# The guard's count and its comparison, issued two steps behind the sums that they use

## The chip, the cores and the metric

The kernel runs on one core of one Trainium2 chip. The metric is the device time of one execution in microseconds; lower is better. Engines are named as in the profile: PE (TensorE matmul) and PEld (its weight loads), DVE (VectorE), ACT (ScalarE), POOL (GpSimd), SP (SyncE, which issues most DMAs).

## The reference

Three blocks follow each other: an attention with a window and sink positions, a gated feed-forward block with a short convolution along the sequence, and an attention with four experts of which two are weighted per position.

```python
scores = np.where(is_sink | in_window, scale * q @ k.T, -1e9)   # 2 x 8 heads, 768 positions, 64 wide
x = softmax(scores) @ v                                          # n_sink 4, window 128
h = np.maximum(x @ w_in, 0.0)                                    # 512 -> 1024
conv_out = sum(conv_w[k] * shifted(h, k - 1) for k in range(3))
y = h * sigmoid(conv_out) @ w_out                                # 1024 -> 512
for e in range(4):                                               # causal attention of each expert
    a = softmax(causal(scale * (y @ wq[e]) @ (y @ wk[e]).T))
    out += weight_of_the_two_best(y @ w_gate, e) * (a @ (y @ wv[e]) @ wo[e])
```

`w_in`, `conv_w` and `w_out` come as 64-bit floats, the rest as 32-bit floats. `n_sink` and `window` are inputs too.

## The kernel before, in words

All work is laid out for 128 partitions. The first attention goes over two batches of 6 row tiles and 4 pairs of heads (lines 450 to 640). The feed-forward block follows in steps: for batch 0 three chunks of 256 positions in two halves of the hidden tiles, for batch 1 two chunks of 384 positions over 8 hidden tiles `f`. The last block makes queries, keys and values (lines 922 and 991) and then goes over 6 row tiles and 2 pairs of experts for each batch (lines 1040 to 1136).

One step of the feed-forward block in batch 1 is this chain, which is spread over four steps of the program (`LAGM`):

- `m1_H` (line 768): 12 matmuls of 128x386 into one PSUM buffer `psB`; ACT takes it out with the relu (L774) and multiplies the middle tap (L776).
- `m1_conv`: DVE adds the two outer taps (L785, L786), ACT takes the tanh (L788).
- `m1_gate`, one step later: DVE multiplies (L794), ACT copies a rounded half `g[0]` (L800). `m1_rest`, another step later: POOL makes the remainder `g[1]` (L806).
- `m1_Y` (line 822), three steps behind `m1_H`: 12 matmuls of 128x384 that add `w_out` times `g` into four PSUM buffers, which are held over the 8 hidden tiles.

In each step the program order is given by the string `ORD1`: `rest`, `H`, `gate`, `Y`, `conv` and then `z.misc`, which is the function `misc` of `mlp_phase`. Each engine works through its own list in program order. There are 8 PSUM buffers `psB`, handed out in turn; with four held by `m1_Y`, four go round.

The 64-bit weights are turned into 32-bit floats on the chip by a short sequence that is right only for magnitudes under a bound. While it reads the weights, ACT sums their scaled magnitudes into the columns of the tile `guard`, 128 x 17 (L340). When the last weights are done, at step `w0` of the feed-forward block, `misc` calls `narrow`: DVE compares the 17 columns with the bound (L189) and adds up each row into `g` (L190), PE adds up the 128 rows with a matmul of `g` against a column of ones (L192, 1x1 output), and DVE compares the result with 128 x 17 and multiplies by the verdict on `n_sink` and `window` (L193) into `flag`. The flag is read once, at the end of the program: if it is 0, a general version of the whole program runs as well.

In the same step `misc` then lays out the buffers for the weights of the last block and issues their first load (L888, one in each of 8 steps).

Of the kernel before, what the change touches and what calls it, by code (L numbers as in the profile page):

```python
# [89 lines left out]
class Kernel:  # L90
# [94 lines left out]
    def narrow(self):  # L185

        nc = self.nc
        g, ok = self.sm(1, "g"), self.guard
        nc.vector.tensor_scalar(ok, ok, GUARD, None, op0=ALU.is_lt)  # L189
        nc.vector.tensor_reduce(g, ok, axis=AX.X, op=ALU.add)  # L190
        ps = self.psB()[0:1, 0:1]
        nc.tensor.matmul(ps, g, self.ones, start=True, stop=True)  # L192
        nc.vector.scalar_tensor_tensor(self.flag[0:1], ps, float(P * (2 * NF + 1)), self.inside[0:1, 0:1], op0=ALU.is_ge, op1=ALU.mult)  # L193

    def indices(self):
# [669 lines left out]
    def mlp_phase(self, start):  # L865
        nc = self.nc
        self.m1h, self.m1g = {}, {}
        hf = NF // 2 if self.halves else NF
        steps = [(0, c, f) for f0 in range(0, NF, hf) for c in range(NCH) for f in range(f0, f0 + hf)]
        steps1 = [(1, c, f) for c in range(NT // TPC[1]) for f in range(NF)]  # L870
        w0 = NSTEP + NF // 2

        def misc(i):
            self.tail_step()
            self.background(BG2 // 2)
            if i == w0 and self.halves:
                self.narrow()
            if i == w0:
                hi = self.Kt([P, NKC, WQKV], F32R, "wqh")
                self.wq_ = ([hi[:, :, lo:up] for lo, up in WCOLS], [self.Rt([P, NKC, up - lo], s="wql") for lo, up in WCOLS])  # L880
            if w0 <= i < w0 + 2 * NKC:
                n = i - w0
                raw = self.Wt([P, DM], s="raw")
                kc = n // 2
                groups = (2,) if n % 2 else (0, 1)
                lo, up = WCOLS[groups[0]][0], WCOLS[groups[-1]][1]
                raw = raw[:, : up - lo]
                nc.sync.dma_start(raw, self.wqkv[kc * P : (kc + 1) * P, lo:up])  # L888
                self.wraw[n] = [(raw[:, WCOLS[g][0] - lo : WCOLS[g][1] - lo], *(w[g][:, kc] for w in self.wq_)) for g in groups]
            if w0 + 2 <= i < w0 + 2 + 2 * NKC:  # L890
                for part in self.wraw.pop(i - w0 - 2):
                    self.hilo_later(*part)

        def more(i):
            self.tail_step()
            self.background(BG2 // 2)

        def phase(start, steps, lags):
            def each(fn):
                return lambda i: fn(*steps[i])  # L900

            conv, gate, rest, Y = lags
            st = {"rest": (rest, each(self.m1_rest)), "gate": (gate, each(self.m1_gate)), "conv": (conv, each(self.m1_conv)),
                  "H": (0, each(self.m1_H)), "Y": (Y, each(self.m1_Y))}
            return lambda names: (start, len(steps), [st[n] for n in names.split()], 1)

        n0 = start + len(steps)
        total = len(steps) + len(steps1)
        z = {"more": (0, more), "misc": (0, misc)}
        return (phase(start, steps, LAGM[0]), phase(n0, steps1, LAGM[1]),  # L910
                lambda names: (start, total, [z[n] for n in names.split()], 1), start + total)
# [422 lines left out]
```

## Time and profile before

| | |
|---|---|
| time, median of 3 runs | 377.04 us (376.21 to 377.78) |
| the profiled execution's own time | 375.66 us |
| its span, from the first to the last instruction | 373.7 us |
| TensorE's granted clock over the span, mean | 0.995 of full speed |
| PE busy | 360.1 us (96%), 2974 instructions |
| PEld busy | 331.8 us (89%) |
| DVE busy | 276.4 us (74%) |
| ACT busy | 257.8 us (69%) |
| POOL busy | 118.8 us (32%) |

Times in the trace are counted from the start of the span. A group of matmuls is read best by the start of its first and the start of the next group's first, since ends of matmuls are modelled. The clock is given as the share that the throttle granted: 1.00 is 2.4 GHz, 0.50 is 1.2 GHz. An idle time in square brackets stands before the instruction and names what ended it.

### The profile page before, as it was taken

To read this page: it belongs to the slowest core of one execution; us is meant where nothing else is said; L and a number is where in the kernel's file an instruction comes from. 1 tells how busy PE (TensorE), PEld (TensorE's weight loads), DVE (VectorE), ACT (ScalarE), POOL (GpSimd) and SP (SyncE) were. 2 spreads that over 40 slices of the span, in tenths; PEclk is the share of its full clock that TensorE was granted. 3 is DMA by queue.
4 is the path that set the end of the run, shared out by engine and by line. 5 is a ranking of instruction groups with operands and counts; after the bars stand their busy time and mean duration, and the time that the engine had idled before them with its cause. 6 is when DMAs were issued, how large, how long until landed. Compare 5 with 4: busy or idle time off the path is not lost.

```text
span 373.7 us, 8472 instructions
## 1 busy us (share of the span) xinstructions
PE 360.1 (96%) x2974; PEld 331.8 (89%) x2974; DVE 276.4 (74%) x843; ACT 257.8 (69%) x731; POOL 118.8 (32%) x224
## 2 busy tenths in 40 slices
PE   7999999899999999999699999999999999999995
PEld 5687777899889999999699999999999899978984
DVE  5689898999887987777837577457678697668731
ACT  4999998767877776446435655449869687839841
POOL 7013111444332352843512212410025134505320
PEclk9999999999999999999989999999999999999999
DMA  7944865363332300001101101000000000101012
GB/s 181 356 140 121 251 203 172 114 198 114 119 109 81 91 29 31 16 14 31 42 16 46 39 3 53 5 1 2 2 0 4 0 30 30 56 3 59 30 59 92
DMA packets 20402, 27.49 MB, mean 74 GB/s; under 512 B 2080, under 2 KB 12416, under 8 KB 20352
## 3 DMA queue, kind: packets, MB, share of 16 engines
q1 hardware_dynamic: 19120, 26.22, 22.0%
q10 hardware_dynamic: 1232, 0.66, 0.9%
q8 instruction: 25, 0.41, 0.4%
q14 instruction: 25, 0.20, 0.2%
HBM read 23.68 MB, written 3.19 MB: 72 GB/s over the span
## 4 chain that ended last, share of the span: by engine, by line
PE 67%; DVE 19%; ACT 6%; issue 3%; POOL 2%; DMA 1%; ACTq 0%; DVEq 0%; POOLq 0%
PE psB L822 12%; PE psB L768 10%; PE psB L991 9%; PE psB L1107 5%; PE psB L1083 5%; PE psB L922 5%; PE psB L1131 4%; PE psB L588 4%; PE psB L485 3%; DVE P L487 3%; PE psB L546 3%; PE psB L1054 2%; PE psB L1053 2%; DVE ht L786 2%; DVE ht L785 2%
## 5 line engine op out<-in xcount | busy, mean ns | idle before, releaser
L822 PE MATMUL psB<-g,wouthf 128*128 128x256 f32 (+1 forms) x320 | 68.5, 304 | 0.2 <-POOL g L806 0.2
L1071 POOL TENSOR_SCALAR P<-P,r 128x256 f32<-128x256 f32 (+5 forms) x48 | 30.1, 641 | 79.8 <-DVE r L1069 32.7
L490 ACT ACTIVATE P<-P,nm 128x260 f32<-128x260 f32 (+2 forms) x96 | 46.4, 486 | 10.9 <-DVE nm L487 10.8
L822 PEld LDWEIGHTS psB<-g,wouthf 128*128 128x128 f32 x320 | 52.8, 188 | 0.9 <-POOL g L806 0.7
L822 PE MATMUL psB<-g,woutlf 128*128 128x256 f32 (+1 forms) x160 | 48.4, 303 | 0.0
L1060 ACT ACTIVATE P<-P,nm 128x256 f32<-128x256 f32 (+5 forms) x48 | 32.1, 670 | 13.4 <-DVE nm L1059 7.8
L768 PE MATMUL psB<-xh,winhf 128*128 128x258 f32 (+1 forms) x128 | 40.8, 319 | 0.1
L768 PE MATMUL psB<-xh,winlf 128*128 128x258 f32 (+1 forms) x128 | 38.5, 301 | 0.0
L768 PE MATMUL psB<-xl,winhf 128*128 128x258 f32 (+1 forms) x128 | 38.5, 301 | 0.0
L778 POOL TENSOR_SCALAR ht<-ht,cw 128x256 f32<-128x256 f32 x24 | 15.1, 630 | 62.4 <-ACT ht L774 56.2
L1056 DVE CUSTOM_DVE_ANT_0 P<-psB,causal 128x384 f32<-128x384 f32 (+3 forms) x64 | 30.2, 502 | 5.7 <-PE psB L1054 5.3
L806 POOL TENSOR_TENSOR g<-t,g 128x384 fp32r<-128x384 f32 x16 | 17.0, 1065 | 48.4 <-ACT g L800 36.3
L822 PEld LDWEIGHTS psB<-g,woutlf 128*128 128x128 f32 x160 | 30.1, 188 | 0.0
L546 PE MATMUL psB<-ident,P 128*128 128x128 f32 x176 | 29.1, 281 | 0.4 <-ACT P L490 0.2
L991 PE MATMUL psB<-yh,wqh 128*128 128x256 f32 x96 | 27.2, 283 | 0.0
L991 PE MATMUL psB<-yh,wql 128*128 128x256 f32 x96 | 27.0, 281 | 0.0
L991 PE MATMUL psB<-yl,wqh 128*128 128x256 f32 x96 | 26.9, 281 | 0.0
L502 ACT COPY PT<-psB 128x512 f32<-128x512 f32 (+1 forms) x48 | 25.5, 531 | 0.8 <-PE psB L546 0.8
L768 PEld LDWEIGHTS psB<-xh,winhf 128*128 128x128 f32 x128 | 24.8, 194 | 0.6 <-ACT ht L774 0.4
L788 ACT ACTIVATE t<-t 128x384 f32<-128x384 f32 x16 | 8.4, 525 | 24.3 <-DVE t L786 24.3
L768 PEld LDWEIGHTS psB<-xl,winhf 128*128 128x128 f32 x128 | 24.7, 193 | 0.0
L768 PEld LDWEIGHTS psB<-xh,winlf 128*128 128x128 f32 x128 | 24.6, 192 | 0.0
(198 smaller groups left out, 1030.5 us busy)
## 6 DMA issues: line engine op xcount, KB each, us to landing
raw<-in_w_in_dram SPq DMA_DIRECT2D x8, 512.0 KB, 4.7
raw<-in_w_out_dram SPq DMA_DIRECT2D x8, 512.0 KB, 3.4
v<-in_v_dram SPq DMA_DIRECT2D x12, 256.0 KB, 4.5
R<-rD SPq DMA_DIRECT2D x24, 128.0 KB, 3.1
out_dram<-ot SPq DMA_DIRECT2D x11, 256.0 KB, 2.0
k<-in_k_dram SPq DMA_DIRECT2D x7, 260.0 KB, 3.9
q<-in_q_dram SPq DMA_DIRECT2D x6, 256.0 KB, 4.0
k<-in_k_dram SPq DMA_DIRECT2D x2, 520.0 KB
```

What stands on the lines that cost most here:

```text
L490: nc.scalar.activation(Pt[:, j, :N], Pt[:, j, :N], AF.Exp, bias=nmx[:, j : j + 1], scale=-1.0, accum_out=sums[:, j : j + 1])
L502: self.nc.scalar.copy(dst, src)
L546: nc.tensor.transpose(ps[:, j, c, :], Pt[:, j, c0 : c0 + P], self.ident)
L768: nc.tensor.matmul(ps[:, : n + 2], w[:, f, kc, :], x[kc], start=(i == 0), stop=(i == len(ops) - 1))
L822: nc.tensor.matmul(self.m1y[d // per][:, d % per, :], w[:, f, d, :], g[k], start=(first and i == 0 and d % per == 0), stop=(last and i == ...
L922: nc.tensor.matmul(ps[:, :NVG], y[:, kc, ts_], w[2][:, kc], start=(i == 0), stop=(i == len(ops) - 1))
L991: nc.tensor.matmul(ps, w[which][:, kc, cols], y[:, kc, :], start=(i == 0), stop=(i == len(ops) - 1))
L1056: nc.vector.tensor_tensor_reduce(out=Pt[:, lo:hi], in0=ps[:, : hi - lo], in1=mask, scale=-1.0, scalar=BIG, op0=ALU.add, op1=ALU.min, accum ...
L1060: nc.scalar.activation(Pt[:, :N], Pt[:, :N], AF.Exp, bias=nm[:, 0:1], scale=-1.0, accum_out=sums[:, j : j + 1])
L1071: nc.gpsimd.tensor_scalar(Ps[j][:, :N], Ps[j][:, :N], r[:, j : j + 1], 1.0, op0=ALU.mult, op1=ALU.mult)
L1083: nc.tensor.transpose(ps[:, s, :], Ps[j][:, c * P : (c + 1) * P], self.ident)
L1107: nc.tensor.matmul(o[j * D : (j + 1) * D, p, :], self.v2[(b, c)][:, e * D : (e + 1) * D], where[(j, c)], start=(c == 0), stop=(c == qt), s ...
```

## The change

`narrow` keeps the two DVE instructions and remembers `g`. The matmul and the comparison become a function of their own, `decide`, which `misc` calls at step `w0 + 2`. Nothing is added or left out: the numbers of instructions on every engine stay as they were. All lines behind the edit count 5 more in the changed file (7 more behind the second edit).

```diff
         nc.vector.tensor_scalar(ok, ok, GUARD, None, op0=ALU.is_lt)
         nc.vector.tensor_reduce(g, ok, axis=AX.X, op=ALU.add)
+        self.within = g
+
+    def decide(self):
+
+        nc = self.nc
         ps = self.psB()[0:1, 0:1]
-        nc.tensor.matmul(ps, g, self.ones, start=True, stop=True)
+        nc.tensor.matmul(ps, self.within, self.ones, start=True, stop=True)
         nc.vector.scalar_tensor_tensor(self.flag[0:1], ps, float(P * (2 * NF + 1)), self.inside[0:1, 0:1], op0=ALU.is_ge, op1=ALU.mult)
...
             if i == w0 and self.halves:
                 self.narrow()
+            if i == w0 + 2 and self.halves:
+                self.decide()
```

PE's list at step `w0` before: the end of one `m1_Y` group, the count's matmul, the start of the next `m1_H` group.

```order
L822 MATMUL psB_2741<-g_2682,wouthf 128x384
L822 MATMUL psB_2741<-g_2681,woutlf 128x384
L192 MATMUL psB_2801<-ones,g_2798 1x1
L768 MATMUL psB_2811<-xh_1244,winhf 128x386
L768 MATMUL psB_2811<-xl_1246,winhf 128x386
```

PE's list at the same place in the changed kernel.

```order
L827 MATMUL psB_2741<-g_2682,wouthf 128x384
L827 MATMUL psB_2741<-g_2681,woutlf 128x384
L773 MATMUL psB_2808<-xh_1244,winhf 128x386
L773 MATMUL psB_2808<-xl_1246,winhf 128x386
L773 MATMUL psB_2808<-xh_1244,winlf 128x386
```

And two steps on, where the count's matmul now stands.

```order
L827 MATMUL psB_2741<-g_2778,wouthf 128x384
L827 MATMUL psB_2741<-g_2779,wouthf 128x384
L827 MATMUL psB_2741<-g_2778,woutlf 128x384
L197 MATMUL psB_2883<-ones,g_2798 1x1
L773 MATMUL psB_2891<-xh_1244,winhf 128x386
L773 MATMUL psB_2891<-xl_1246,winhf 128x386
```

On PE the count's matmul has moved behind 48 other matmuls: the `m1_H` group (now into `psB_2808`), the `m1_Y` group on `g_2719`, the next `m1_H` group and the `m1_Y` group on `g_2778`.

DVE's list before, from the last taps ahead of the two sums on (`t` and `h` are tiles of one hidden tile `f` each).

```order
L786 SCALAR_TENSOR_TENSOR t_2774<-h_2773,cw,t_2774 128x384
L189 TENSOR_SCALAR guard<-guard 128x17
L190 TENSOR_REDUCE g_2798<-guard 128x1
L193 SCALAR_TENSOR_TENSOR flag<-psB_2801,c_831 1x1
L794 SCALAR_TENSOR_TENSOR t_2774<-t_2774,h_2773 128x384
```

DVE's list in the changed kernel.

```order
L791 SCALAR_TENSOR_TENSOR t_2774<-h_2773,cw,t_2774 128x384
L189 TENSOR_SCALAR guard<-guard 128x17
L190 TENSOR_REDUCE g_2798<-guard 128x1
L799 SCALAR_TENSOR_TENSOR t_2774<-t_2774,h_2773 128x384
L790 SCALAR_TENSOR_TENSOR t_2822<-h_2821,cw,t_2822 128x384
L791 SCALAR_TENSOR_TENSOR t_2822<-h_2821,cw,t_2822 128x384
L799 SCALAR_TENSOR_TENSOR t_2822<-t_2822,h_2821 128x384
L790 SCALAR_TENSOR_TENSOR t_2861<-h_2860,cw,t_2861 128x384
L791 SCALAR_TENSOR_TENSOR t_2861<-h_2860,cw,t_2861 128x384
L198 SCALAR_TENSOR_TENSOR flag<-psB_2883,c_831 1x1
L799 SCALAR_TENSOR_TENSOR t_2861<-t_2861,h_2860 128x384
```

On DVE the two sums stay where they were; the comparison has moved behind six instructions. On ACT, POOL and SP the order of the instructions is unchanged.

## Rows read from the trace of the kernel before

**Rows 1.** The page: engines over the span, and the granted clock in 40 slices.

```profile
PE 360.1 (96%) x2974; PEld 331.8 (89%) x2974; DVE 276.4 (74%) x843; ACT 257.8 (69%) x731; POOL 118.8 (32%) x224
...
PEclk9999999999999999999989999999999999999999
```

**Rows 2.** The chain of waits that ended last, around 186 us: start us, us, what.

```profile
185.34 0.18 DVE g L190
185.66 0.19 PE psB L192 x2
185.85 3.70 PE psB L768 x12
189.54 2.10 PE psB L822 x12
191.64 2.14 PE psB L768 x12
```

**Rows 3.** PE's waits over the span: line, releaser, total us, times, longest us.

```profile
PE psB L192 <- DVE g L190: 2.9, 1, 2.9
PE psB L515 <- DVE su L498: 1.8, 4, 1.0
```

**Rows 4.** Timeline of DVE: start us, us, engine, line, operation, tiles, count, [idle before].

```profile
180.02 1.54 DVE L786 SCALAR_TENSOR_TENSOR t<-h,cw,t 128x384 f32<-128x384 f32 x1
...
185.34 0.17 DVE L190 TENSOR_REDUCE g<-guard 128x1 f32<-128x17 f32 x1
...
191.47 1.28 DVE L786 SCALAR_TENSOR_TENSOR t<-h,cw,t 128x384 f32<-128x384 f32 x1
```

**Rows 5.** Timeline of PE, the same columns: first and last matmuls of the groups.

```profile
178.14 0.34 PE L822 MATMUL psB<-g,woutlf 128*128 128x384 f32 x1
178.32 0.34 PE L768 MATMUL psB<-xh,winhf 128*128 128x386 f32 x1
...
180.45 0.51 PE L822 MATMUL psB<-g,wouthf 128*128 128x384 f32 x2
...
182.38 0.34 PE L822 MATMUL psB<-g,woutlf 128*128 128x384 f32 x1
...
185.66 0.19 PE L192 MATMUL psB<-ones,g 128*1 128x1 f32 x2 [2.94 <-DVE g L190]
185.78 0.69 PE L768 MATMUL psB<-xh,winhf 128*128 128x386 f32 x1
...
189.38 0.51 PE L822 MATMUL psB<-g,wouthf 128*128 128x384 f32 x2
...
195.72 0.34 PE L768 MATMUL psB<-xh,winhf 128*128 128x386 f32 x1
```

**Rows 6.** L768 by stretches: us, PE busy (count), PEld busy (count), granted clock, DMA share, GB/s.

```profile
178.30:180.45 2.15, 2.13 (x12) 1.99 (x12) 1.00 0.01 4
185.78:189.38 3.60, 3.60 (x12) 3.44 (x12) 0.57 0.00 0
```

**Rows 7.** The instructions of L192: count, duration in ns min/median/max, first and last start.

```profile
L192 PEld LDWEIGHTS psB<-ones,g x2: 79/80/81, 185.6 to 185.7; 128*1 128x1 f32 x2
L192 PE MATMUL psB<-ones,g x2: 163/163/163, 185.7 to 185.7; 128*1 128x1 f32 x2
```

**Rows 8.** Timelines of ACT and POOL, columns as for DVE.

```profile
182.03 0.48 ACT L774 ACTIVATE h<-psB 128x386 f32<-128x386 f32 x1
...
185.26 0.52 ACT L788 ACTIVATE t<-t 128x384 f32<-128x384 f32 x1 [1.52 <-DVE t L786]
...
183.82 0.99 POOL L806 TENSOR_TENSOR g<-t,g 128x384 fp32r<-128x384 f32 x1 [1.09 <-ACT g L800]
191.32 1.02 POOL L806 TENSOR_TENSOR g<-t,g 128x384 fp32r<-128x384 f32 x1 [6.51 <-issue]
```

**Rows 9.** All engines by stretches: us, busy (count) of PE, PEld, DVE, ACT, POOL, clock, DMA.

```profile
260.00:330.00 70.00, 69.92 (x631) 67.21 (x629) 50.87 (x204) 55.22 (x152) 21.20 (x36) 1.00 0.04 16
330.00:373.70 43.70, 38.89 (x350) 33.92 (x348) 26.30 (x103) 26.05 (x63) 12.06 (x18) 0.99 0.14 51
```

## The prediction

> **What bounds the kernel now.** I read the page first, then the chain of waits, PE's waits, the stretches, and last the timelines around the edit. On the page PE is busy for 96% of the span, PEld for 89%, DVE for 74% [rows 1]. Modelled ends make a busy PE look fuller than it is, so this alone proves no bound. The chain of waits does more: it passes through exactly the two instructions that the edit parts. It goes from DVE's row sum (L190) to the count's matmul (L192), and from there over PE alone, group after group of L768 and L822 [rows 2]. PE's waits say what that costs: the matmul waited 2.9 us for L190, once, and this is PE's longest wait in the whole span; the next in total, L515, has 1.8 us in four pieces of at most 1.0 [rows 3].
>
> Why DVE was late: the two sums stand in its list behind taps that took long here. The tap L786 at 180.02 took 1.54 us [rows 4]; the row sum came only at 185.34. PE had issued its last L822 matmul at 182.38 and stood until 185.66 [rows 5]. The operands of the matmul group behind it, xh, xl and weights, were long on the chip: the group waits only because it stands behind the count in PE's list.
>
> The second cost stands right behind. One slice of the granted clock shows an 8 between nines [rows 1]. The L768 group behind the count, 12 matmuls like every other, ran at a mean clock of 0.57 and took 3.60 us from 185.78 to 189.38; its neighbour before took 2.13 us at 1.00 [rows 5, 6]. The level fell to 0.50 (1.2 GHz) after PE had stood for 2.94 us.
>
> **The change, step by step.**
>
> 1. The pause goes. A first L768 matmul starts 0.18 us after the last L822 of the group before (178.14 to 178.32) [rows 5]. Without the count in between the group starts at 182.38 + 0.18 = 182.56 instead of 185.78: 3.22 us.
>
> 2. The slow group goes. Without a pause PE stays at 1.00, and the group takes 2.13 us (178.32 to 180.45) instead of 3.60: 1.47 us [rows 5, 6]. Together 4.69 us.
>
> 3. The count's matmul comes back two steps on, with its two weight loads and two passes. No row shows it inside a running stream. From below: in its place now it starts 0.12 us before the next group (185.66 to 185.78) [rows 5]. From above: its four records end to end, 2 x 0.080 + 2 x 0.163 = 0.49 us [rows 7]. I take 0.20, nearer the lower end, because there too the next group's first matmul had started before the two passes' 0.33 us were over. It cannot wait for its input: g is ready at 185.34 + 0.17 = 185.51, and the matmul comes at 182.56 + 2.13 + 2.10 + 2.13 + 2.10 = 191.02 (two pairs of groups; an L822 group takes 2.10 in the chain) [rows 2, 4, 5].
>
> 4. The comparison on DVE moves behind six instructions, to behind the taps of the H group that now ends near 188.92. Before, such taps ended 191.47 + 1.28 - 189.38 = 3.37 us after the next L822 group began [rows 4, 5]; now that is 188.92 + 3.37 = 192.29. The count is through PE near 191.2, some 1.1 us earlier, so DVE does not wait for it. Behind the comparison stands the gate's multiplication, which waits for ACT's tanh anyway. Cost: nothing; if the cover fails, DVE is late by what the matmul is late.
>
> 5. PSUM. The count takes its buffer two steps later, so the H group takes the one that the count had. It waits for an eviction by ACT; even the latest relu ahead of it ended at 182.03 + 0.48 = 182.51, before 182.56 [rows 8]. Cost: nothing, at worst about 0.1 us.
>
> 6. What is late next. With the pause gone PE runs into its L822 groups 3 to 4.7 us earlier. The one at 184.69 uses a g whose remainder POOL made before the one of 183.82. The one at 188.92 uses that of 183.82 + 0.99 = 184.81: 4 us early. The one at about 193.35 uses the remainder that stood at 191.32 before. That date was set by the slow H group: ACT does the relu and the tap of the H group ahead of the copy. Now ACT is free for the relu at 185.26 + 0.52 = 185.78, then relu, tap and copy (0.5, 0.6, 0.5) and POOL's 1.0 make 188.4: 5 us early [rows 8]. So the chain of a hidden tile does not become the bound.
>
> 7. ACT, POOL and SP keep their lists. The loads of the last block's weights wait for buffers that PE and DVE free, so they go out earlier with them; in a stretch with a DMA share near 0 they meet nothing.
>
> Sum: 3.22 + 1.47 - 0.20 = 4.49 us. It can be set beside another reading: the group after the count's new place would start at 191.22 instead of 195.72 [rows 5], 4.50 us. From there to 330 us PE has almost no idle time (0.08 us between 260 and 330), and in the last 43.7 us it has 4.8 [rows 9]. All that PE or DVE wait for there is itself fed by PE, so I let the whole 4.5 us through to the end.
>
> The profiled execution takes 375.66 us and would take 371.2. It lies 1.4 us under the median of the three runs, 377.04, and I take the difference off the median: **372.5 us**.
>
> A rule that speaks against term 2. The row shows a fall in one execution, with matmuls that really spread out (2.13 to 3.60 us for 12) [rows 6]. The Trainium skill, "TensorE: Matmul & The Clock Gate", Part 1, says that low is the default and activity releases it, but also that where the level changes is "run-variable". By that a timed run of the kernel before need not hold the fall at all, the sum would be 3.22 - 0.20 = 3.02 us, and that is the first rival below; no row here shows a second execution.
>
> **The rivals.**
>
> - *Only the pause is worth something.* In the timed runs the clock does not fall after the pause, or it falls elsewhere in the changed kernel too. Then 3.22 - 0.20 = 3.02 us: 374.0. For it: one execution alone shows the fall, and there are other idle times in which the clock held 1.00 [rows 3, 9]. Against it: those pauses are at most 1.0 us long in PE's waits, and a run without the fall would be 1.5 us shorter than the profiled one, near 374.2; the three runs lie at 376.21 and above. 20%.
> - *A new wait takes the place of the old.* PE, 4.5 us earlier, meets a late POOL remainder or PSUM eviction in the next steps, stands as long there, and the clock falls there. That returns 2.94 + 1.47 of the 4.7: about 376.8, no difference that can be measured. It decides if the chain of step 6 is 5 us longer than I worked out. DVE's long taps beside POOL speak for it, the slack of 4 and 5 us against. 6%.
> - *Slower: the comparison holds up DVE.* It now stands in the middle of DVE's taps, behind a matmul that stands behind an L822 group. If DVE reaches it before that matmul, DVE stands, the gate, ACT's copy and POOL's remainder come late, and PE pauses at its next L822 groups. It decides when DVE is ahead by more than the 1.1 us of step 4 and then late by more than the 5 us of step 6. One pause with its fall of the clock (4.4 us) only eats the gain; with two the time is 377.04 - 4.5 + 8.8 = 381.3. 2%.
> - That the change does not do what it says is excluded by the order shown: the count stands behind 48 matmuls.
>
> **How the numbers follow.** The forecast has 72%, the rivals 20, 6 and 2. A measurement here can tell about 0.5%, 1.9 us, so faster is below 375.15: 0.92; within 0.06; slower 0.02. The low end takes the sum with the count at its lower bound, 4.57 us, from the fastest run, 376.21: 371.6. The high end takes the first rival with the count at its upper bound, 3.22 - 0.49 = 2.73 us, from the slowest run, 377.78: 375.0. That holds the forecast and most of the first rival, and leaves out the other two and some scatter.
>
> **What would show it.** Right: PE's wait at the count is gone, no L768 group is longer than about 2.2 us, the granted clock is 1.00 from 182 to 200 us, the count starts near 191 us and costs the stream 0.1 to 0.5 us, the first L768 matmul behind it starts near 191.2, and the last L1131 group comes about 4.5 us earlier. Wrong in part: a clock row of 0.50 somewhere else (term 2), a wait of PE on L806 or L774 between 182 and 200 us (step 6), a wait of DVE at the comparison (step 4), or a lead at 195 us that is gone by the end, which would say that the last block waits for something that PE does not feed.

## The result, and the profile after

| | before | changed kernel |
|---|---|---|
| time, median of 6 runs each, same chip | 376.6 us (376.09 to 377.78) | 371.72 us (371.06 to 372.44) |
| ratio | | 0.9867, 95% interval 0.9847 to 0.9887 |
| the profiled execution's own time | 375.66 us | 372.16 us |
| its span | 373.7 us | 370.3 us |
| mean granted clock over the span | 0.995 | 0.998 |
| PE busy | 360.1 us | 359.7 us |

The kernel became faster, by the mechanism that was forecast. 371.72 lies at the low end of the range (371.6 to 375.0), and the ratio applied to 376.6 gives 371.59, which is just under it. The gain is 5.0 us by the ratio (4.3 to 5.8), where 4.5 was forecast. Executions far off the rest are left out of every figure below: one of the kernel before (500.54 us) and two of the filled pause (397.29 and 893.30 us).

PE's waits in the trace of the changed kernel, all that are listed (columns as in [rows 3]). The wait at the count, 2.9 us before, is gone and no line has taken its place; what is left was there before, within 0.1 us.

```profile
PE psB L520 <- DVE su L503: 1.9, 4, 1.0
PE psB L244 <- DVE zeros L238: 1.0, 1, 1.0
PE psB L593 <- ACT PT L507: 0.7, 1, 0.7
PE psB L490 <- DMA k<-in_k_dram: 0.6, 1, 0.6
PE psB L601 <- DVE SPT L580: 0.4, 1, 0.4
PE psB L1138 <- DVE zl L132: 0.3, 1, 0.3
PE psB L827 <- POOL g L811: 0.2, 1, 0.2
```

PE's timeline in the changed kernel, which answers to [rows 5]. This execution is 0.53 us later than the one of before already at 157 us, so differences are read, not dates.

```profile
182.91 0.34 PE L827 MATMUL psB<-g,woutlf 128*128 128x384 f32 x1
183.08 0.34 PE L773 MATMUL psB<-xh,winhf 128*128 128x386 f32 x1
...
185.21 0.51 PE L827 MATMUL psB<-g,wouthf 128*128 128x384 f32 x2
...
191.36 0.34 PE L827 MATMUL psB<-g,woutlf 128*128 128x384 f32 x1
191.63 0.19 PE L197 MATMUL psB<-ones,g 128*1 128x1 f32 x2
191.75 0.44 PE L773 MATMUL psB<-xh,winhf 128*128 128x386 f32 x1
```

The next group starts 0.17 us after the last L827 matmul (182.91 to 183.08), and takes 2.13 us (to 185.21). From the last L827 matmul ahead of the old place of the count to the first L773 behind its new place it took 195.72 - 182.38 = 13.34 us before [rows 5] and takes 191.75 - 182.91 = 8.84 us now: 4.50 us.

The stretches of the three L773 groups, to be read against [rows 6]: two at their usual length, and the one behind the count 0.1 us longer.

```profile
183.08:185.21 2.13, 2.13 (x12) 1.96 (x12) 1.00 0.45 121
187.29:189.43 2.14, 2.13 (x12) 1.97 (x12) 1.00 0.00 0
191.75:193.99 2.24, 2.24 (x12) 2.08 (x12) 1.00 0.42 117
```

DVE's timeline: the comparison follows the taps at once, with no idle time in front of it.

```profile
191.67 1.29 DVE L791 SCALAR_TENSOR_TENSOR t<-h,cw,t 128x384 f32<-128x384 f32 x1
192.88 0.14 DVE L198 SCALAR_TENSOR_TENSOR flag<-psB,c 1x1 int32<-1x1 f32 x1
193.55 0.56 DVE L799 SCALAR_TENSOR_TENSOR t<-t,h 128x384 f32<-128x384 f32 x1 [0.53 <-ACT t L793]
```

Two pieces of the chain of waits, first of the kernel before, then of the changed kernel: a group of the first attention, and PE's last group.

```profile
156.75 1.90 PE psB L588 x32
...
366.23 3.01 PE psB L1131 x18
```

```profile
157.28 1.90 PE psB L593 x32
...
362.31 3.02 PE psB L1138 x18
```

Between them it took 209.48 us before and 205.03 us now: 4.45 us. The lead won at the count reaches PE's last group whole. The profiled executions differ by only 3.5 us, because this one began 0.53 us late and has a longer end behind PE's last matmuls.

### The profile page after: what moved, and what is told of

It reads as the page before. It is cut to its first block, busy times and chain, and to the rows that moved or that the text cites. A ratio compares the mean times of both kernels' runs of the same rounds, so it can differ in the third digit from the quotient of the medians.

```text
span 370.3 us, 8472 instructions
## 1 busy us (share of the span) xinstructions
PE 359.7 (97%) x2974; PEld 332.1 (90%) x2974; DVE 276.8 (75%) x843; ACT 257.7 (70%) x731; POOL 118.8 (32%) x224
## 4 chain that ended last, share of the span: by engine, by line
PE 75%; DVE 14%; ACT 4%; issue 3%; POOL 2%; DMA 1%; SPq 0%; ACTq 0%; DVEq 0%; POOLq 0%
PE psB L827 15%; PE psB L773 13%; PE psB L998 9%; PE psB L1114 5%; PE psB L1090 5%; PE psB L929 5%; PE psB L490 4%; PE psB L1138 4%; PE psB L593 4%; PE psB L551 3%; DVE P L492 3%; PE psB L1061 3%; PE psB L1060 3%; DVE ht L791 2%; PE psB L477 1%
## 5 line engine op out<-in xcount | busy, mean ns | idle before, releaser
L827 PE MATMUL psB<-g,wouthf 128*128 128x256 f32 (+1 forms) x320 | 68.4, 304 | 0.2 <-POOL g L811 0.2
L827 PEld LDWEIGHTS psB<-g,wouthf 128*128 128x128 f32 x320 | 52.8, 188 | 0.9 <-POOL g L811 0.7
L827 PE MATMUL psB<-g,woutlf 128*128 128x256 f32 (+1 forms) x160 | 48.4, 303 | 0.0
L773 PE MATMUL psB<-xh,winhf 128*128 128x258 f32 (+1 forms) x128 | 40.2, 314 | 0.1
L773 PE MATMUL psB<-xh,winlf 128*128 128x258 f32 (+1 forms) x128 | 38.0, 297 | 0.0
L773 PE MATMUL psB<-xl,winhf 128*128 128x258 f32 (+1 forms) x128 | 37.9, 296 | 0.0
L811 POOL TENSOR_TENSOR g<-t,g 128x384 fp32r<-128x384 f32 x16 | 17.0, 1064 | 44.0 <-ACT g L805 35.8
L827 PEld LDWEIGHTS psB<-g,woutlf 128*128 128x128 f32 x160 | 30.1, 188 | 0.0
L490 PE MATMUL psB<-k,q 128*128 128x260 f32 (+2 forms) x96 | 24.9, 389 | 0.6 <-DMA k<-in_k_dram 0.6
L773 PEld LDWEIGHTS psB<-xh,winhf 128*128 128x128 f32 x128 | 24.3, 190 | 0.6 <-ACT ht L779 0.4
L773 PEld LDWEIGHTS psB<-xl,winhf 128*128 128x128 f32 x128 | 24.3, 190 | 0.0
```

The lines of the kernel that those rows point to most:

```text
L490: nc.tensor.matmul(dst, t["q", qt][:, pr, j, :], rhs, start=True, stop=True)
L773: nc.tensor.matmul(ps[:, : n + 2], w[:, f, kc, :], x[kc], start=(i == 0), stop=(i == len(ops) - 1))
L827: nc.tensor.matmul(self.m1y[d // per][:, d % per, :], w[:, f, d, :], g[k], start=(first and i == 0 and d % per == 0), stop=(last and i == ...
```

## The experiments

**Both kernels again.** No edit.

> The kernel before, unchanged, as the yardstick of the other three. Ratio to itself 1.000. If the pause at the count makes the clock fall in every execution (the theory of the prediction), its runs have mean granted clocks near 0.995 and the trace has a stretch at 0.50 behind L192, as in the first profile. If the fall is a matter of chance (first rival), some of its runs have a clock of 0.998 or above and are 1 to 1.5 us shorter than the others.

> The changed kernel again, for a closer ratio. Theory of the prediction: 4.5 us less than before, ratio 0.988. First rival (only the pause counts): 3.0 us, 0.992. If the first measurement (0.9867) is right at its middle, the gain is 5.0 us and 0.5 us of it has another source than the pause, the slow group and the count.

Measured: the kernel before against itself 0.9987 (0.9962 to 1.0012); the changed kernel 371.74 us, ratio 0.9863 (0.9832 to 0.9894). Sorted by the mean clock that each run lists, the 37 executions of the kernel before in this comparison fall into three groups; the changed kernel's 12, of both measurements, stand beside them:

| mean granted clock | executions | mean time |
|---|---|---|
| before, 0.999 and 1.000 | 4 | 374.86 us |
| before, 0.992 to 0.995 | 25 | 376.35 us |
| before, 0.982 to 0.988 | 8 | 377.96 us |
| changed kernel, 0.996 to 1.000 | 12 | 371.78 us |

The mean clock is not the fall at the count alone. In both traces of the changed kernel the clock is under 1.00 only behind PE's last matmul, where it costs nothing (0.60 between 368 and 370 us in the first, with PE idle). The trace of the kernel before in this comparison, with a mean of 0.992, has one fall of 3.4 us at the count, like the first profile with 0.995; the rest lies behind PE's last matmul too. So the groups are a coarse sorting.

Neither theory holds for all executions. With no fall the gain is 374.86 - 371.78 = 3.08 us, what the first rival said (3.02). With the fall that the first profile showed it is 4.57, the forecast (4.49). And in 8 of 37 the clock cost about 3.1 us, twice the priced 1.47. These eight are two sorts: four with 0.987 or 0.988 take 377.52 us on average (2.7 us more than without a fall), four with 0.982 or 0.983 take 378.40 (3.5 more). The mean over the 37, 376.54, gives 4.76 us. Of 14 further executions of the kernel before, in a later comparison on another chip, none has a mean clock above 0.995.

The trace of the kernel before in this comparison shows a further thing. PE's wait at the count ended at 186.28, but the clock fell only some 1.6 us later, when PE was already at work: a mean of 0.94 over the first 1.90 us leaves 0.23 us at 0.50, so the fall began near 187.87 (columns as in [rows 9]):

```profile
186.20:188.10 1.90, 1.82 (x11) 1.82 (x12) 0.61 (x2) 0.20 (x1) 0.00 (x0) 0.94 0.00 0
188.10:191.50 3.40, 3.40 (x13) 3.40 (x12) 0.73 (x2) 1.51 (x3) 0.27 (x1) 0.53 0.00 0
191.50:195.00 3.50, 3.50 (x22) 3.50 (x21) 1.72 (x2) 0.92 (x2) 0.74 (x1) 1.00 0.16 38
```

**The pause filled with work.** The kernel before, with matmuls that nothing uses in the pause; the count overwrites their result.

```diff
-        ps = self.psB()[0:1, 0:1]
+        ps = self.psB()
+        for _ in range(12):
+            nc.tensor.matmul(ps, self.win[0][:, 0, 0, :], self.win[0][:, 0].rearrange("p a c -> p (a c)"), start=True, stop=True)
+        ps = ps[0:1, 0:1]
         nc.tensor.matmul(ps, g, self.ones, start=True, stop=True)
```

> Before, with 12 matmuls of 128x512 of weights against themselves put ahead of the count, in the pause, into the count's PSUM buffer; the count writes over them. PE works for some 2.6 of the 2.94 us and still waits for g. Theory: the pause stays, the clock does not fall, and the L768 group behind takes 2.13 us again: 1.5 us less than before, ratio 0.996. Rival (the fall of the clock costs nothing, or comes from something else than the pause): ratio 1.000, and the group still takes 3.6 us.

Measured: 374.93 us, ratio 0.9947 (0.9926 to 0.9969). The interval leaves out 1.000, the rival. Its 11 executions have mean clocks of 0.997 to 1.000 and take 374.91 us on average, as the four executions of the kernel before without a fall do (374.86). So it is the pause without work that the clock falls after: with matmuls in it 11 of 11 executions show no fall, without them 4 of 37. And the pause alone, with no fall, is worth 374.91 - 371.78 = 3.13 us.

The kept trace is of the execution of 397.29 us, which ran at a granted clock of 0.85 nearly throughout, so the forecast 2.13 us can't be read there. It does show that the L771 group behind the count keeps the pace of its neighbour: 2.37 us, where the group before the fill took 2.27 (187.09 to 189.36). At that clock the twelve matmuls lasted until 194.72 while `g` was ready at 193.14, so PE met no wait for `g`. That they end before `g` is ready at 1.00 is an estimate: 3.10 us times 0.85 is 2.6 us, against 2.94.

```profile
191.62 3.17 PE L193 MATMUL psB<-winhf 128*128 128x512 f32 x12
194.72 0.19 PE L195 MATMUL psB<-ones,g 128*1 128x1 f32 x2
194.84 0.44 PE L771 MATMUL psB<-xh,winhf 128*128 128x386 f32 x1
...
197.21 0.54 PE L825 MATMUL psB<-g,wouthf 128*128 128x384 f32 x2
```

**Sums late too.** The kernel before, with all of `narrow` at step `w0 + 2`.

```diff
-            if i == w0 and self.halves:
+            if i == w0 + 2 and self.halves:
                 self.narrow()
```

> Sums, count and comparison all two steps later, so that the distance between sums and count is nothing again, at the place of the changed kernel. Theory (distance is what counts): PE comes to the count at about 191.5 us and g is ready only after DVE's taps, near 193.2: a pause of 1.7 us; gain over before 4.5 - 1.7 = 2.8 us, ratio 0.9925, if the clock holds over that pause, and some 1.4 us, ratio 0.996, if it falls. Rival (the place is what counts, step w0 is crowded on DVE): no pause, ratio as in the changed kernel, 0.988.

Measured: 373.74 us, ratio 0.9925 (0.99 to 0.9949). PE's wait at the count is there again, now at the new place, and as long as worked out:

```profile
PE psB L192 <- DVE g L190: 1.7, 1, 1.7
```

So the distance counts, not the place. Both forecasts for the clock came true, as far as the mean clocks tell, in different executions: seven of nine have clocks of 0.996 and above and take 373.17 to 374.05, two have 0.993 and take 375.46 and 375.61. The profiled one is of the two; its clock fell 0.7 us after the wait had ended, for 3.4 us:

```profile
191.60:193.20 1.60, 0.00 (x0) 0.00 (x0) 1.48 (x3) 0.34 (x1) 0.81 (x1) 1.00 0.37 70
193.20:194.00 0.80, 0.74 (x5) 0.74 (x6) 0.51 (x2) 0.78 (x3) 0.00 (x0) 1.00 0.49 187
194.00:197.40 3.40, 3.40 (x13) 3.40 (x12) 0.77 (x3) 0.23 (x1) 0.00 (x0) 0.50 0.02 5
```

**One step instead of two.** The changed kernel with `decide` a step earlier.

```diff
-            if i == w0 + 2 and self.halves:
+            if i == w0 + 1 and self.halves:
                 self.decide()
```

> The changed kernel with count and comparison one step behind the sums instead of two. Theory (all that matters is that g is ready when PE comes to the count): PE comes there at about 187 us, g has been ready since some 185.9, no pause; the time of the changed kernel, 371.7, ratio to before 0.987, clock of every execution 0.996 or above. Rival (the second step was needed, since DVE runs late here): a pause of up to 1 us at the count, 372.5 or more.

Measured: 371.83 us, ratio 0.9876 (0.9853 to 0.9898), as the changed kernel. The count stands in the stream without a wait:

```profile
188.14 0.34 PE L827 MATMUL psB<-g,woutlf 128*128 128x384 f32 x1
188.41 0.19 PE L197 MATMUL psB<-ones,g 128*1 128x1 f32 x2
188.53 0.45 PE L773 MATMUL psB<-xh,winhf 128*128 128x386 f32 x1
```

One step is enough; the second neither costs nor brings anything that can be measured. The profiled execution, 372.82 us with a clock of 0.995 where 0.996 or above was expected, had a fall of the clock in the first attention, far from the count: 3.4 us from 59.9 us on, with a wait of PE of 1.24 us for DVE (at L601) that had ended at 58.08. A fall elsewhere happens, but none of the other four has a mean under 0.997.

**The same remedy at the next wait.** The changed kernel, with the transpose of the reciprocal sums in batch 0 (a matmul too) one step later.

```diff
-LAGS = ((1, 2, 1, 4, 3, 4, 5, 5, 2, 7, 7, 9, 11)
+LAGS = ((1, 2, 1, 4, 3, 4, 5, 5, 3, 7, 7, 9, 11)
```

> The changed kernel, and in batch 0 of the first attention the transpose of the reciprocal row sums (the matmul that waits for L498 in four executions of it, 1.8 us in total) one step later: the same remedy at the next largest wait of PE. Theory (a matmul that waits at the head of PE's list holds up all that is behind it): up to 1.8 us less than the changed kernel, 370 to 371.5. Rival (that stage is not bound by PE, the chain there goes over DVE and ACT): the same time as the changed kernel, 371.7, with the wait moved to another line.

Measured: 373.38 us, ratio to before 0.9919 (0.9894 to 0.9945): not faster than the changed kernel, and 1.6 us above its 371.74 by the medians. PE's wait for DVE's row sums (L503) is down to two pieces, but almost as long in total:

```profile
PE psB L520 <- DVE su L503: 1.6, 2, 1.3
```

The pieces that are left are not those that the edit moves. The transpose runs twelve times, six times for batch 0 and then six for batch 1. The four that wait in the changed kernel, and the two that wait in this run:

```profile
13.65 0.27 PE L520 MATMUL psB<-ident,su 128*8 128x128 f32 x1 [0.40 <-DVE su L503]
37.34 0.27 PE L520 MATMUL psB<-ident,su 128*8 128x128 f32 x1 [0.23 <-DVE su L503]
59.43 0.27 PE L520 MATMUL psB<-ident,su 128*8 128x128 f32 x1 [0.30 <-DVE su L503]
72.46 0.27 PE L520 MATMUL psB<-ident,su 128*8 128x128 f32 x1 [1.01 <-DVE su L503]
```

```profile
59.68 0.27 PE L520 MATMUL psB<-ident,su 128*8 128x128 f32 x1 [0.30 <-DVE su L503]
72.98 0.27 PE L520 MATMUL psB<-ident,su 128*8 128x128 f32 x1 [1.29 <-DVE su L503]
```

Those at 13.65 and 37.34 are the first and the fourth of batch 0, and their wait, 0.63 us together, went. Those at 59.43 and 72.46 are the first two of batch 1, whose lag stayed as it was. In this run the six of batch 0 come 0.9 to 2.7 us later than in the changed kernel, the six of batch 1 only 0.2 to 0.6 us. So the expectation was wrong to count 1.8 us: the edit could reach about 0.6 us of it. That much came back at another place, in two waits that the changed kernel does not list:

```profile
PE psB L490 <- DMA q<-in_q_dram: 0.3, 1, 0.3
PE psB L477 <- DMA q<-in_q_dram: 0.3, 1, 0.3
```

At a group of the feed-forward block in the stage behind, the chain of waits of this kernel has no lead over the changed kernel's; the rows are this kernel's, then the changed kernel's:

```profile
106.89 1.69 PE psB L773 x12
```

```profile
106.34 1.71 PE psB L773 x12
```

The remedy took away the waits that it moved, and the time did not follow: the rival's result, with the wait moved to another line. Its reason, a chain over DVE and ACT, is not shown. The larger wait, 1.0 us in batch 1, was never moved, and why the times of this kernel scatter more (372.04 to 375.82) was not tried further.

**Two more executions of the kernel before.** No edit.

> The kernel before, one look, to catch an execution with a mean clock under 0.99. 8 of 37 executions of the kernel before had one and were 1.6 us longer on average than those near 0.995; none of 23 executions of the changed kernel and of the filled pause had. Theory: in such an execution the clock falls behind the count for longer than 3.4 us or twice in a row. Rival: the second fall lies elsewhere and has nothing to do with the count.

> As the look before: the kernel before again, for an execution with a mean clock under 0.99. The same two theories.

Measured: 378.14 us with a mean clock of 0.987, and 374.9 us with 0.999. The first has what the theory asks for. Its timeline around the count and its stretches:

```profile
185.88 0.19 PE L192 MATMUL psB<-ones,g 128*1 128x1 f32 x2 [2.96 <-DVE g L190]
186.00 0.69 PE L768 MATMUL psB<-xh,winhf 128*128 128x386 f32 x1
...
190.02 0.84 PE L822 MATMUL psB<-g,wouthf 128*128 128x384 f32 x2
...
193.07 0.34 PE L768 MATMUL psB<-xh,winhf 128*128 128x386 f32 x1
```

```profile
185.30:192.10 6.80, 6.22 (x21) 6.22 (x22) 1.62 (x6) 2.03 (x4) 0.11 (x1) 0.50 0.00 0
192.10:200.00 7.90, 7.90 (x47) 7.90 (x46) 4.62 (x8) 3.46 (x8) 1.93 (x2) 1.00 0.20 52
```

One fall, 6.8 us long, which began 0.6 us before the wait at the count ended: the L768 group takes 4.02 us, and the L822 group behind it 3.05 instead of 2.10. Together that is 2.8 us over the usual 2.13 and 2.10, about what the four executions at 0.987 and 0.988 showed (2.7). The second has the same wait and no fall at all:

```profile
185.79 0.19 PE L192 MATMUL psB<-ones,g 128*1 128x1 f32 x2 [2.95 <-DVE g L190]
185.91 0.44 PE L768 MATMUL psB<-xh,winhf 128*128 128x386 f32 x1
...
188.14 0.51 PE L822 MATMUL psB<-g,wouthf 128*128 128x384 f32 x2
```

```profile
185.90:188.10 2.20, 2.20 (x14) 2.19 (x13) 0.61 (x2) 0.01 (x1) 0.00 (x0) 1.00 0.00 0
```

Its group takes 2.23 us. So the same pause, within 0.02 us, is followed by a fall of 0, 3.4 or 6.8 us, and the time of the execution goes with it. No trace is of an execution at 0.982 or 0.983, which take another 0.9 us; whether their fall at the count is longer still, or a second one lies elsewhere, is not shown.

## What failed in the prediction, and what held

- **Step 1, the pause (3.22 us): right.** The wait is gone, and the L773 group starts 0.17 us behind the L827 group. With the count's price off, the term stood at 3.02; executions without a fall of the clock show 3.08, the filled pause 3.13 (the means scatter by some tenths).
- **Step 2, the slow group (1.47 us): the step that failed, by its size.** The mechanism holds: filling the pause takes the fall away. But 1.47 was read from one execution and used as if it were the price of every one. In the 37 executions it was about 0 in 4, 1.5 in 25 and 3.1 in 8: on average 376.54 - 374.86 = 1.68. The average is near, the spread is not: the range let this term be 0 or 1.47 and never more. With the pause at 3.08 the mean gain is 4.76 where 4.49 was added up, and the measured time lies at the low end of the range and not in its middle. The gain by the ratio, 5.0, has an interval (4.3 to 5.8) that holds both, so what lies between 4.76 and 5.0 is not told apart from scatter; and that the ratio's 371.59 falls under the low end by 0.01 us is chance. The low end also left no room for the scatter of the changed kernel itself, 371.06 to 372.89 over 12 executions. The first rival took the fall for a matter of chance, which it is, but priced only its absence.
- **The rule set against term 2.** The Trainium skill, "TensorE: Matmul & The Clock Gate", Part 1, says "run-variable" of the rise at a kernel's start, of how many matmuls pass before it. For the fall, which the prediction took it to cover, the runs show the like: one kernel, one pause of 2.9 to 3.0 us, and traces with no fall, with one of 3.4 and with one of 6.8 us. No fall, the 3.02 us of the first rival, happened in 4 executions of 37.
- **Step 3, the count in the stream (0.20 us, between 0.12 and 0.49): right in kind, a little low.** The gap in front of the L773 group is 0.39 us instead of 0.17, and the group itself 2.24 instead of 2.13: 0.33 us. The reading at 195.72, which sees only the gap, came out at 4.50 as worked out.
- **Step 4, the comparison on DVE: right.** The taps end and the comparison starts at 192.88, 0.53 us being this execution's later date, against 192.29 worked out; no idle time in front of it. The slower case had nothing to stand on.
- **Steps 5 to 7: right.** No wait of PE on an eviction between 182 and 200 us, none on L811 that was not there before; the lead of 4.5 us reaches PE's last group at 4.45 us.
- **The base.** The median of the first three runs, 377.04, was 0.4 us above that of six, 376.6. Of the 0.8 us between 372.5 and 371.72 the base is about half, step 2 by its average 0.2 us, and the rest lies within the scatter.

What stays open: what decides, from one execution to the next, how long the fall is.

## What to carry to other kernels

An instruction that takes another engine's result stands best where that result is long there: at the head of an in-order list it holds up everything behind it, however small it is, and distance in the list cost nothing that could be measured here (371.83 us with one step, 371.74 with two). On PE the price of a pause is the pause plus what the clock takes behind it, and the second part differs between executions; price it from several, by the clock of each, with an upper end for the longest fall seen. Before the remedy is used again, see which executions of the waiting line it moves, and what PE meets next: at the reciprocal sums it reached 0.6 us of a wait of 1.8, and as much came back at loads of `q`.

## What the runs showed of the hardware that was not expected

- After the same wait of PE (2.94 to 2.96 us) the clock stood at 1.2 GHz for 0, 3.4 or 6.8 us in different executions.
- The fall need not begin in the pause. In the first profile it began at 185.5 us, 0.2 us before the count's matmul; in another it came 1.6 us after the wait, in the midst of matmuls.
- A pause of 1.7 us was followed by a fall in two of nine executions, one read in the trace and one by its mean clock of 0.993. With the 2.9 us pause 33 of 37 had a mean clock that tells of one.
- A fall of 3.4 us began 1.8 us after a wait of PE of only 1.24 us had ended, in one execution (one step instead of two). That the wait caused it is not shown.
